# Reversing the order of the key chunks in the later passes of P V, in a fused attention and gated feed-forward kernel

## Chip, cores and metric

The kernel runs on one core of one Trainium2 chip. The metric is device time in microseconds (us), the median of several executions.

## What is computed

Block-causal attention (blocks of 64 positions) over a batch of 8, with 8 heads of size 64 and 576 positions, followed by a feed-forward layer whose hidden signal is gated by a convolution of width 3:

```
scores = np.where(block_i >= block_j, scale * q @ k.T, -1e9)
attn = exp(scores - max) / (sum + 1e-09)
x = (attn @ v) with the 8 heads side by side        # 576 x 512 for each batch
h = np.maximum(x @ w_in, 0.0)                       # 512 -> 1024
out = (h * sigmoid(conv3(h)) ) @ w_out              # 1024 -> 512
```

All is float32. The kernel reaches that precision with float32r matmuls by splitting an operand into a high part and a low part (the remainder) and adding the products of the parts.

## The kernel before

**Heads.** Heads are worked on in pairs, a "visit". The first batch is visited twice, once for its queries 0 to 255 (part "A") and once for its queries 256 to 575 (part "B"). The 28 pairs of the seven other batches are visited once, with all 576 queries (part None, "full-width" below). For each head: scores by 128 queries (L707 to L747), exponential and normalisation, transposes of the probabilities (L791), and then the product P V (L868), which is where the change is.

**Tiles of P V.** The transposed probabilities lie in `ptah` and `ptal` (high and low part, queries 0 to 255) and in `ptbh` and `ptbl` (queries 256 to 575). In `ptbh[:, c, :]` the 128 partitions are the keys of chunk c (c = 0 to 3, 128 keys each) and the 320 columns are queries 256 to 575. Only the last 64 queries see the last 64 keys (512 to 575). For them the corner of `ptbh` that chunk 3 leaves unused, `ptbh[:, 3, 0:64]`, is used: its partitions 0 to 63 hold the high part and 64 to 127 the low part. The values lie in `vv`, where the last 64 keys stand twice, in partitions 0 to 63 and 64 to 127 of chunk 4; columns 0 to 63 of `vv` are the high part ("h") and 64 to 127 the low part ("l"); "a" is both, 128 columns.

**Passes.** `stage_pv` makes a block of queries in one PSUM bank `tb` (tag "w" in the profile), by passes over the chunks. For a full-width head there are two passes: "a" with the high part of P (the stationary operand is `vv`, 128 columns wide) and "h" with the low part of P (64 columns wide). Parts A and B make three: "h", "l" with the high part of P, and "h" with the low part, all 64 columns wide. The stationary operand is loaded anew for each matmul. A full-width head has two blocks: queries 0 to 255 (chunks 0 and 1, moving 256 and 128 columns) and queries 256 to 575 (chunks 0 to 2 with 320 columns each, chunk 3 with 192). Before the change each pass goes from chunk 0 to the last, and the product of the last 64 keys (64 moving columns, the "tail", L875) stands right behind chunk 0 of each pass but the last. In the "l" pass of part B it reads 64 partitions in place of 128.

**Order of the work.** Nothing is ordered by the engines themselves. Every operation is given to a planner, `Plan.order`, with an engine, an assumed duration, a due time and what it depends on. The planner simulates the five engines, always takes the operation that can start first (due times break ties), and so writes out one fixed order for each engine. A pass over a block is one operation; for queries 256 to 575 it is cut in two halves, chunks 0 and 1, and chunks 2 and 3. The matmuls of the feed-forward layer (L936, L993) are "paced" operations which fill TensorE between the steps of the attention. Where the planner finds TensorE idle for longer than 0.45 us it inserts transposes of the identity (L1110) whose results nobody reads. The assumed duration of a matmul with n moving columns and m columns of stationary operand is `max(n / 2240, 2 * m / 2400) + 0.003` us. The waits between engines follow from what the instructions read and write, not from the planner's dependences.

Of the kernel before, what the change touches and what calls it, by code (L numbers as in the profile page):

```python
# [193 lines left out]
def kernel(  # L194
# [10 lines left out]
    nc = tc.nc  # L205
    B, H, S, D = q.shape
    DM, DFF = w_in.shape
    KC = conv_w.shape[0]
    P = 128
# [46 lines left out]
    def bank(tag):  # L256
        tag = {"tv": "w", "pt": "w"}.get(tag, tag)
        return pl.buf(psum[tag], [P, 512], F32, tag, NBANK[tag])
# [22 lines left out]
    def c_mm(n, m=P):  # L281
        return max(n / 2240.0, 2 * m / 2400.0) + 0.003

    def c_act(n, psum=True, ap=False, acc=False):
        return (0.051 if psum else 0.093) + n / 1200.0 + (0.093 if ap else 0) + (0.08 if acc else 0)

    def c_dve(n, fast=False, two_in=False):
        return 0.065 + n / (1920.0 if fast else 960.0) + (0.05 if two_in else 0.0)
# [559 lines left out]
    def stage_pv(vvd, hh, xt, x, at, part, chunk=lambda c: c, xx=None):  # L848
        early = part is not None
        vv, vdone = vvd  # L850
        o64 = 64 * hh
        done = []
        passes = (("h", 64, 0), ("l", 64, 0), ("h", 64, 1)) if early else (("a", P, 0), ("h", 64, 1))
        w = {"h": slice(0, D), "l": slice(D, P), "a": slice(0, P)}
        for qa, qb in {None: ((0, 256), (256, S)), "A": ((0, 256),), "B": ((256, S),)}[part]:
            tb = bank("tv")
            n = qb - qa
            pts = x[0] if qa == 0 else x[1]
            cs = [c for c in range(4) if 128 * c < qb]
            need = x[2] if qa == 0 else x[3]  # L860
            o = None
            for k, (ps_, m, lo) in enumerate(passes):
                halves = [cs] if qa == 0 else [cs[:2], cs[2:]]
                for z, half in enumerate(halves):
                    def mm(ps_=ps_, m=m, pm=pts[lo], pth=pts[0], half=half, k=k, tb=tb, qa=qa, qb=qb, cs=cs):
                        for c in half:
                            q0 = max(128 * c, qa)
                            nc.tensor.matmul(tb.ap[0:m, q0 - qa:qb - qa], vv.ap[:, chunk(c), hh, w[ps_]],  # L868
                                             pm.ap[:, 128 * c + q0:128 * c + qb] if qa == 0 else pm.ap[:, c, q0 - qa:],
                                             start=(k == 0 and c == 0),  # L870
                                             stop=(k == len(passes) - 1 and c == cs[-1]), skip_group_check=True)

                            if c == 0 and k < len(passes) - 1 and qb == S:
                                r = P if ps_ != "l" else 64
                                nc.tensor.matmul(tb.ap[0:m, 512 - qa:S - qa], vv.ap[0:r, 4, hh, w[ps_]],  # L875
                                                 pth.ap[0:r, 3, 0:64], start=False, stop=False, skip_group_check=True)

                    cost = sum(c_mm(qb - max(128 * c, qa), m) for c in half) + (c_mm(64, m) if k == 0 and 0 in half else 0)
                    deps = [o] + vdone + ([e[0] for e in need] if k == 0 else [])
                    deps += [e[1] for e in need] if lo else []  # L880
                    if qb == S:
                        deps += [need[-1][1]]
                    o = pl.op(PE, cost, mm, at + (0.3 if qa else 0), deps=deps, bufs=[vv, tb] + pts)

            def ev0(tb=tb, qa=qa, qb=qb, n=n):
                nc.scalar.activation(out=xt.ap[o64:o64 + 64, qa:qb], in_=tb.ap[0:64, 0:n], func=AF.Copy)  # L886

            def ev3(tb=tb, qa=qa, qb=qb, n=n):
                nc.vector.tensor_tensor(out=xt.ap[o64:o64 + 64, qa:qb], in0=tb.ap[64:128, 0:n],  # L889
                                        in1=xt.ap[o64:o64 + 64, qa:qb], op=ALU.add)  # L890

            def evh(tb=tb, qa=qa, qb=qb, n=n):
                nc.scalar.activation(out=xx[0].ap[o64:o64 + 64, qa:qb], in_=tb.ap[0:64, 0:n], func=AF.Copy)

            def evl(tb=tb, qa=qa, qb=qb, n=n):
                nc.vector.tensor_tensor(out=xx[1].ap[o64:o64 + 64, qa:qb], in0=tb.ap[0:64, 0:n],
                                        in1=xx[0].ap[o64:o64 + 64, qa:qb], op=ALU.subtract)

            if xx:
                o = pl.op(ACT, c_act(n) + 0.08, evh, at + 0.6, deps=[o], bufs=[tb, xx[0]])  # L900
                done.append(pl.op(DVE, c_dve(n, two_in=True) + 0.02, evl, at + 1.0, deps=[o], bufs=[tb] + list(xx)))
                continue
            o = pl.op(ACT, c_act(n) + 0.08, ev0, at + 0.6, deps=[o], bufs=[tb, xt])
            if not early:
                o = pl.op(DVE, c_dve(n, two_in=True) + 0.07, ev3, at + 1.0, deps=[o], bufs=[tb, xt])
            done.append(o)
        return done
# [164 lines left out]
    for i, (p, part) in enumerate(visits):  # L1072
# [8 lines left out]
        for hh in range(2):  # L1081
            n = 2 * i + hh
            b0 = base[n]
            sm = stage_s(ops, hh, b0, part, None)
            if hh == 0 and i + 1 < len(visits):
                nops = transposes(i + 1, b0 + ot)
                if i + 2 < len(visits) and i + 2 > NP:
                    fetch(i + 2, b0 + ot + NLEAD)
            x = stage_x(sm, hh, b0 + ox, part, x[4] if x else None)
            es += stage_pv(vvd[i], hh, xt, x, b0 + opv, part, (lambda c, p=p: 2 * (p % 2) + c) if part == "A" else lambda c: c, xs[p][:2] if part and XDIRECT else None)  # L1090
# [5 lines left out]
        if p % NP == NP - 1:  # L1096
            xb = [(xs[z][0], xs[z][1], list(xs[z][2])) for z in range(b * NP, b * NP + NP)]
            c = base[2 * i + 2] + opv + (OFA if part == "A" else OFB if part else OF)
# [4 lines left out]
            else:  # L1103
                for half in range(2):
                    c = ffn(b, HS * half, HS * half + HS, xb, c, H * SLOT / 2)
# [40 lines left out]
```

## Time and profile before

| | us |
|---|---|
| median of 3 runs | 825.06 (824.58 to 827.27) |
| the profiled execution's own time | 826.01 |
| its span, from the first to the last instruction | 824.2 |
| TensorE busy in it | 805.8 (98%) |

Busy times are those of the profile. A matmul's recorded duration runs from its start to the end of its results and overlaps the next one; how fast matmuls follow each other is read from their starts.

### The profile page before, as it was taken

What the parts mean: (1) busy time and instruction counts of PE and PEld (TensorE: products, weight loads), DVE (VectorE), ACT (ScalarE), POOL (GpSimd) and SP (SyncE); (2) the same over time, 40 slices, a digit from 0 to 9 for tenths busy, and PEclk for the clock granted to TensorE, in tenths of its full rate; (3) what the DMA queues carried; (4) which work ended last, traced back from release to release, by engine and by line L of the source; (5) the groups of instructions that cost most, each with busy time, mean ns of one, the idle gap of its engine ahead of it and who ended that gap; (6) DMA issues with size and microseconds to landing.
All of it is one profiled execution on the core that took longest, in us unless ns stands there. A gap on an engine that the chain in (4) does not pass through costs nothing.

```text
span 824.2 us, 17518 instructions
## 1 busy us (share of the span) xinstructions
PE 805.8 (98%) x5531; PEld 736.6 (89%) x5531; DVE 658.5 (80%) x1945; ACT 634.0 (77%) x1800; POOL 437.9 (53%) x579
## 2 busy tenths in 40 slices
PE   7999899999999999999999999999999999999997
PEld 6888778988999989999999989999999989999996
DVE  5899887998997967889797967889797977887541
ACT  5789887887896967878796967878796967877651
POOL 2456566564565645546555645546565645645421
PEclk9999999999999999999999999999999999999999
DMA  9364756556555544444556444445556434430001
GB/s 234 113 155 104 183 159 157 131 126 147 146 119 145 117 103 107 106 113 114 145 119 146 108 113 103 106 114 117 145 119 144 116 91 113 93 99 14 14 26 40
DMA packets 168096, 96.09 MB, mean 117 GB/s; under 512 B 136748, under 2 KB 142404, under 8 KB 168004
## 3 DMA queue, kind: packets, MB, share of 16 engines
q1 hardware_dynamic: 165924, 94.44, 47.3%
q8 instruction: 45, 0.74, 0.4%
q10 hardware_dynamic: 2080, 0.52, 0.4%
q14 instruction: 47, 0.39, 0.2%
HBM read 38.82 MB, written 9.44 MB: 59 GB/s over the span
## 4 chain that ended last, share of the span: by engine, by line
PE 90%; DVE 3%; SPq 2%; ACT 2%; DMA 2%; issue 1%; POOL 0%; ACTq 0%; DVEq 0%
PE f L936 24%; PE f L993 21%; PE w L868 12%; PE w L791 10%; PE s L709 5%; PE s L711 5%; PE w L582 4%; PE w L993 3%; PE s L747 3%; PE s L936 2%; PE s L1110 1%; DMA xh<-in_moe_w_out_dram 1%; SPq L372 1%; DMA kn<-in_k_dram 1%; DMA ka<-kh 1%
## 5 line engine op out<-in xcount | busy, mean ns | idle before, releaser
L682 POOL TENSOR_SCALAR p<-p,st 128x512 f32<-128x512 f32 (+4 forms) x260 | 144.3, 570 | 158.6 <-DVE st L676 73.1
L974 POOL TENSOR_TENSOR gl<-t,gh 128x288 fp32r<-128x288 f32 (+2 forms) x128 | 103.9, 816 | 127.4 <-ACT gh L971 101.2
L720 ACT ACTIVATE p<-s,st 128x128 f32<-128x128 f32 (+1 forms) x248 | 131.2, 529 | 36.2 <-DVE st L717 31.0
L791 PE MATMUL w<-ident,p 128*128 128x128 f32 (+1 forms) x800 | 126.6, 275 | 1.9 <-DVE kl L589 1.4
L717 DVE TENSOR_REDUCE st<-s 128x1 f32<-128x128 f32 (+1 forms) x248 | 120.4, 486 | 4.0
L801 ACT ACTIVATE ptbh<-w 128x512 fp32r<-128x512 f32 (+2 forms) x192 | 94.5, 509 | 26.5 <-PE w L791 25.5
L791 PEld LDWEIGHTS w<-ident,p 128*128 128x128 f32 (+1 forms) x800 | 95.3, 140 | 12.9 <-ACT p L688 1.9
L993 PE MATMUL f<-woh,gh 128*128 128x512 f32 x248 | 105.8, 427 | 0.0
L936 PE MATMUL f<-xh,wih 128*128 128x290 f32 (+2 forms) x480 | 101.7, 312 | 0.4 <-ACT stage L1003 0.3
L804 DVE TENSOR_TENSOR ptbl<-w,ptbh 128x512 fp32r<-128x512 f32 (+1 forms) x144 | 89.9, 633 | 14.8 <-ACT ptbh L801 14.3
L936 PE MATMUL f<-xh,wil 128*128 128x290 f32 (+2 forms) x480 | 99.2, 310 | 0.0
L993 PE MATMUL f<-woh,gl 128*128 128x512 f32 x248 | 98.2, 396 | 0.0
L993 PE MATMUL f<-wol,gh 128*128 128x512 f32 x248 | 98.1, 395 | 0.0
L936 PE MATMUL f<-xl,wih 128*128 128x290 f32 (+2 forms) x480 | 96.0, 305 | 0.0
L711 PE MATMUL s<-kl,qz 128*128 128x128 f32 (+1 forms) x240 | 78.0, 325 | 0.0
L936 PEld LDWEIGHTS f<-xh,wih 128*128 128x128 f32 x480 | 74.1, 189 | 3.9 <-DVE t L967 0.6
L955 DVE SCALAR_TENSOR_TENSOR t<-f,cw,t 128x287 f32<-128x287 f32 (+3 forms) x120 | 59.0, 492 | 20.6 <-ACT t L951 19.4
L936 PEld LDWEIGHTS f<-xl,wih 128*128 128x128 f32 x480 | 73.8, 190 | 0.8
L936 PEld LDWEIGHTS f<-xh,wil 128*128 128x128 f32 x480 | 73.2, 190 | 0.3
L889 DVE TENSOR_TENSOR xt<-w,xt 64x256 f32<-64x256 f32 x112 | 51.3, 460 | 27.2 <-ACT xt L886 24.6
L886 ACT ACTIVATE xt<-w 64x256 f32<-64x256 f32 x112 | 44.8, 402 | 23.0 <-PE w L868 18.4
L868 PE MATMUL w<-ptbh,vv 128*128 128x320 f32 (+3 forms) x288 | 62.3, 320 | 0.0
(161 smaller groups left out, 2054.7 us busy)
## 6 DMA issues: line engine op xcount, KB each, us to landing
kn<-in_k_dram SPq DMA_DIRECT2D x64, 144.0 KB, 2.9
ka<-kh SPq DMA_DIRECT2D x64, 144.0 KB, 2.7
kb<-kh SPq DMA_DIRECT2D x64, 144.0 KB, 2.6
out_dram<-stage SPq DMA_DIRECT2D x36, 256.0 KB, 2.3
vn<-in_v_dram SPq DMA_DIRECT2D x64, 128.0 KB, 2.6
qn<-in_q_dram SPq DMA_DIRECT2D x56, 144.0 KB, 2.7
qa<-qh SPq DMA_DIRECT2D x28, 144.0 KB, 3.1
qa<-ql SPq DMA_DIRECT2D x28, 144.0 KB, 3.1
```

The lines of the kernel that those rows point to most:

```text
L682: nc.gpsimd.tensor_scalar(out=pt.ap, in0=pt.ap, scalar1=st.ap[:, col:col + 1], scalar2=0.0, op0=ALU.mult, op1=ALU.add)
L711: nc.tensor.matmul(sb.ap[:, 0:nk], qz.ap[:, z:z + 128], kl.ap[:, 0:nk], start=False, stop=True)
L717: nc.vector.tensor_reduce(out=st.ap[:, i:i + 1], in_=sb.ap[:, 0:nk], op=ALU.max, axis=AX.X, negate=True)
L720: nc.scalar.activation(out=pt.ap[:, 0:nk], in_=sb.ap[:, 0:nk], func=AF.Exp, bias=st.ap[:, i:i + 1], accum_out=st.ap[:, 4 + 2 * i:5 + 2 * i])
L791: nc.tensor.matmul(tb.ap[0:kk, col:col + P], pb[x].ap[:, 128 * c:128 * c + kk], ident, start=(z == 0), stop=True, is_transpose=True, skip_ ...
L801: nc.scalar.activation(out=hi(), in_=src(), func=AF.Copy)
L804: nc.vector.tensor_tensor(out=lo(), in0=src(), in1=hi(), op=ALU.subtract)
L868: nc.tensor.matmul(tb.ap[0:m, q0 - qa:qb - qa], vv.ap[:, chunk(c), hh, w[ps_]], pm.ap[:, 128 * c + q0:128 * c + qb] if qa == 0 else pm.ap[ ...
L936: nc.tensor.matmul(fb.ap[:, 0:n2], wt[:, c, fs], xs[c][xi].ap[:, x0:x0 + n2], start=(n + c - c0 == 0), stop=(n + c - c0 == 3 * NCC - 1))
L955: nc.vector.scalar_tensor_tensor(out=t.ap[:, i0:no], in0=fb.ap[:, own + i0 - 1:own + no - 1], scalar=cw[:, f:f + 1], in1=t.ap[:, i0:no], o ...
L974: nc.gpsimd.tensor_tensor(out=gbuf[1].ap[:, f, carry:carry + no], in0=t.ap[:, 0:no], in1=gbuf[0].ap[:, f, carry:carry + no], op=ALU.subtract)
L993: nc.tensor.matmul(fb.ap[:, 0:DM], gbuf[a].ap[:, f, cs], w[:, f, :], start=(f == 0 and n == 0), stop=(f == NFC - 1 and n == 2))
```

## The change

In every pass but the first the chunks are taken from the last to the first, and the halves in reverse as well. The tail no longer stands behind chunk 0 of the same pass. It is the first matmul of the next pass, with the columns of `vv` that belong to the pass before (`wp`, `mp`), and always reads all 128 partitions. The number of matmuls is the same. The planner's durations follow: the tail is counted in the first half of each later pass, where it was counted in the first half of the first pass.

```diff
                 halves = [cs] if qa == 0 else [cs[:2], cs[2:]]
+                if k:
+                    halves = [h[::-1] for h in halves[::-1]]
                 for z, half in enumerate(halves):
-                    def mm(ps_=ps_, m=m, pm=pts[lo], pth=pts[0], half=half, k=k, tb=tb, qa=qa, qb=qb, cs=cs):
+                    tailed = k and z == 0 and qb == S
+                    def mm(ps_=ps_, m=m, pm=pts[lo], pth=pts[0], half=half, k=k, z=z, tb=tb, qa=qa, qb=qb, halves=halves,
+                           tailed=tailed):
+                        if tailed:
+                            wp, mp = passes[k - 1][:2]
+                            nc.tensor.matmul(tb.ap[0:mp, 512 - qa:S - qa], vv.ap[:, 4, hh, w[wp]],
+                                             pth.ap[:, 3, 0:64], start=False, stop=False, skip_group_check=True)
                         for c in half:
                             q0 = max(128 * c, qa)
                             nc.tensor.matmul(tb.ap[0:m, q0 - qa:qb - qa], vv.ap[:, chunk(c), hh, w[ps_]],
                                              pm.ap[:, 128 * c + q0:128 * c + qb] if qa == 0 else pm.ap[:, c, q0 - qa:],
                                              start=(k == 0 and c == 0),
-                                             stop=(k == len(passes) - 1 and c == cs[-1]), skip_group_check=True)
-
-                            if c == 0 and k < len(passes) - 1 and qb == S:
-                                r = P if ps_ != "l" else 64
-                                nc.tensor.matmul(tb.ap[0:m, 512 - qa:S - qa], vv.ap[0:r, 4, hh, w[ps_]],
-                                                 pth.ap[0:r, 3, 0:64], start=False, stop=False, skip_group_check=True)
-
-                    cost = sum(c_mm(qb - max(128 * c, qa), m) for c in half) + (c_mm(64, m) if k == 0 and 0 in half else 0)
+                                             stop=(k == len(passes) - 1 and z == len(halves) - 1 and c == half[-1]),
+                                             skip_group_check=True)
+
+                    cost = sum(c_mm(qb - max(128 * c, qa), m) for c in half) + (c_mm(64, m) if tailed else 0)
```

## Rows read from the trace of the kernel before

**Rows 1.** The page's head and its busy times.

```profile
span 824.2 us, 17518 instructions
...
PE 805.8 (98%) x5531; PEld 736.6 (89%) x5531; DVE 658.5 (80%) x1945; ACT 634.0 (77%) x1800; POOL 437.9 (53%) x579
```

**Rows 2.** Busy time by stretch: stretch, length, engines (instructions), clock, DMA share, GB/s.

```profile
240.00:400.00 160.00, 160.00 (x1087) 146.98 (x1086) 132.45 (x392) 125.19 (x363) 87.81 (x121) 1.00 0.49 117
...
320.00:340.00 20.00, 20.00 (x153) 19.35 (x152) 19.32 (x57) 19.05 (x57) 13.06 (x18) 1.00 0.54 124
```

**Rows 3.** Chain of waits, 240 to 760 us, then 60 to 135 us.

```profile
by line: PE f L936 28.3%; PE f L993 28.3%; PE w L868 13.2%; PE w L791 11.9%; PE s L711 5.4%; PE s L709 5.2%; PE w L582 4.1%; PE s L747 3.5%; PE w L875 0.3%
...
by line: PE w L868 13.4%; PE f L936 10.4%; PE w L791 6.9%; PE s L1110 6.8%; DMA kn<-in_k_dram 5.6%; DMA ka<-kh 5.5%; PE w L808 4.3%; issue 4.0%; PE f L993 3.9%; PE s L747 3.6%; DVE st L717 3.4%; PE s L709 3.3%; PE s L711 2.8%; ACT p L720 2.
...
88.30 4.19 DMA kn<-in_k_dram
```

**Rows 4.** Timeline of TensorE, one full-width head: start, us, instruction, count merged.

```profile
411.64 0.34 PE L868 MATMUL w<-ptal,vv 128*64 128x256 f32 x2
411.81 0.36 PE L868 MATMUL w<-ptbh,vv 128*128 128x320 f32 x1
412.01 0.19 PE L875 MATMUL w<-ptbh,vv 128*128 128x64 f32 x1
412.04 0.62 PE L868 MATMUL w<-ptbh,vv 128*128 128x320 f32 x3
...
412.27 0.40 PE L868 MATMUL w<-ptbh,vv 128*128 128x320 f32 x2
...
412.50 0.69 PE L868 MATMUL w<-ptbl,vv 128*64 128x320 f32 x4
413.03 0.46 PE L936 MATMUL f<-xh,wih 128*128 128x290 f32 x2
...
413.19 0.30 PE L936 MATMUL f<-xh,wih 128*128 128x290 f32 x1
```

**Rows 5.** Timeline of TensorE, another full-width head, between its two blocks.

```profile
423.11 0.49 PE L936 MATMUL f<-xl,wih 128*128 128x290 f32 x2
...
423.30 0.30 PE L936 MATMUL f<-xl,wih 128*128 128x290 f32 x1
423.44 0.32 PE L868 MATMUL w<-ptbh,vv 128*128 128x320 f32 x1
423.59 0.19 PE L875 MATMUL w<-ptbh,vv 128*128 128x64 f32 x1
```

**Rows 6.** Groups of TensorE by form: line, operation, form, count, busy us, mean ns.

```profile
L868 PE MATMUL w<-ptbh,vv 128*128 128x320 f32 x168 | 43.5, 347 | 0.0
L868 PE MATMUL w<-ptbl,vv 128*64 128x320 f32 x192 | 41.1, 312 | 0.0
```

**Rows 7.** Timeline of TensorE, a head of part B.

```profile
106.18 0.19 PE L875 MATMUL w<-ptbh,vv 128*64 128x64 f32 x1
106.21 0.71 PE L868 MATMUL w<-ptbh,vv 128*64 128x320 f32 x4
...
106.38 0.40 PE L868 MATMUL w<-ptbh,vv 128*64 128x320 f32 x2
...
106.61 0.31 PE L868 MATMUL w<-ptbh,vv 128*64 128x320 f32 x1
...
106.85 0.24 PE L875 MATMUL w<-ptbh,vv 64*64 64x64 f32 x1
107.02 0.36 PE L868 MATMUL w<-ptbh,vv 128*64 128x320 f32 x1
107.22 0.38 PE L791 MATMUL w<-ident,p 128*128 128x128 f32 x2
```

**Rows 8.** Timeline of TensorE: transposes, two matmuls of the feed-forward layer, a transpose.

```profile
413.52 0.51 PE L936 MATMUL f<-xh,wil 128*128 128x290 f32 x2
413.87 0.25 PE L582 MATMUL w<-ident,qn 96*128 96x96 f32 x1
```

## The prediction

> **What bounds the kernel now.** I read the page first. TensorE is busy for 98% of the span, and its weight loads (PEld) for 89% [rows 1]. These busy times overlap one another, so they don't say yet that TensorE sets the pace. The busy times by stretch come next: between 240 and 400 us TensorE is busy without a gap at a granted clock of 1.00, which is the 2.4 GHz level, while VectorE has 132 of 160 us and ScalarE 125 [rows 2]. The chain of waits settles it: from 240 to 760 us its named shares are all TensorE's, and 13.2% of it are P V matmuls on L868 [rows 3]. So in the stretch that holds most of the 56 full-width heads, a nanosecond saved on TensorE is a nanosecond of the kernel, as long as the other engines keep their slack. Before 135 us it is different: from 60 to 135 us TensorE's lines share the chain with DMA transfers, VectorE, ScalarE and filler transposes (L1110), and L868 has 13.4% of 75 us [rows 3].
>
> Since matmuls overlap, I read TensorE's pace from starts. What a matmul occupies is the time from its start to the next start, its "slot". In the full-width head of [rows 4], the four matmuls of pass "h" (three of 320 columns, one of 192) take 413.03 - 412.50 = 530 ns. Three of pass "a" (320, 320, 192) take 412.50 - 412.04 = 460 ns, of which the first has 412.27 - 412.04 = 230 and the others 230 together. From 3x + y = 530 and x + y = 230, a slot of 320 columns is 150 ns and one of 192 is 80 ns. The tail has a slot of 412.04 - 412.01 = 30 ns. So the one matmul behind the tail takes 230 in place of 150 ns, 80 too many.
>
> My reading: the next weights are loaded while the current matmul streams, and a matmul waits only for the part of its load that the matmul ahead of it does not cover. Behind a 30 ns tail, 80 ns are uncovered, so a load of 128 columns is about 80 + 30 = 110 ns. This can be tested elsewhere. The two matmuls of 256 and 128 columns in [rows 4] take 411.81 - 411.64 = 170 ns, so some 60 for the shorter one, and behind it a0 takes 412.01 - 411.81 = 200: 50 too many, and 50 + 60 is 110 again. In [rows 5] a0 stands behind a matmul of 290 columns and takes 423.59 - 423.44 = 150: nothing too many. There the feed-forward matmul behind the 128-column one has 423.30 - 423.11 = 190 where the next has 140. The averages agree: the 168 matmuls of 320 columns with 128-column weights last 347 ns, the 192 with 64-column weights 312 [rows 6]. 35 ns times 168 is 5.9 us, and 56 times 80 ns (all a1) plus 30 times 50 ns (the 30 heads whose a0 follows the first block at once) is 6.0 us. A load of 64 columns: the matmul behind part B's first tail takes 106.38 - 106.21 = 170, 20 too many, so about 50 ns.
>
> The Trainium skill ("TensorE: Matmul & The Clock Gate", section "LDWEIGHTS (loading the stationary operand)") gives columns divided by 1.2 in ns, so 107 and 53 ns, whatever the number of rows. The 110 and 50 of the trace agree on columns; by that page's figures the full-width sum below would be within 0.3 us of the one from rows.
>
> **The change, part by part.** No matmul is added or removed; what changes is which load stands behind which stream.
>
> *Full-width heads, queries 256 to 575 (56).* Removed: a1 no longer follows the tail, 80 ns. Added: the tail now follows a3, whose 80 ns cover all but 30 of its 110 ns load: 30 ns. Then h3 follows the tail, with a 64-column load of 50 behind 30: 20 ns. The pass now ends with 320 columns in place of 192, so whatever comes next has its load covered: [rows 4] shows 413.19 - 413.03 = 160 for the next matmul where 140 is normal. That is 20 ns where a matmul with 128-column weights follows, nothing where transposes do; between 0 and 20 I take 15. Net 80 - 30 - 20 + 15 = 45 ns.
>
> *Full-width heads, queries 0 to 255 (56).* Pass "h" now ends with 256 columns in place of 128. a1 and h1 are followed by a 64-column load, which 60 ns cover both ways. Removed is the 50 ns that the next operation waits, whether it is a0 of the other block [rows 4] or a feed-forward matmul [rows 5]. In the timeline 54 of 56 have such a successor; the bounds are 0 and 50, and I take 50.
>
> Together 95 ns times 56 is 5.3 us. All of it is TensorE time on the chain, in the stretch where nothing else is on it.
>
> *Part B (8 heads).* Here the tail of pass "l" reads 64 partitions and its load is not fetched ahead: the matmul before it takes 106.85 - 106.61 = 240 ns (90 too many), the tail itself 107.02 - 106.85 = 170 (140 too many), the matmul behind it 107.22 - 107.02 = 200 (50 too many) [rows 7]. With 128 partitions these 280 ns go. The matmul behind the first tail loses its 20 and two matmuls behind the moved tails gain 20 each, so 260 ns a head, 2.1 us in all. By the skill's rule just named, the number of rows does not matter, and this 2.1 us would be about nothing; the trace differs, with 170 against 30 ns. How much of it is on the path? L868 has 13.4% of 75 us = 10 us of the chain there [rows 3]; eight heads of some 2 us each (14 slots of about 150 ns) are about 17 us. So 0.6 of it: 1.2 us, with bounds 0 and 2.1.
>
> *Part A (8 heads).* At most 50 ns each, at the start, where much else is waited for: 0 to 0.4 us, and I take 0.
>
> *Waits.* The tail reads the last thing that is made of a head's probabilities. It stands later now, so its wait can only get shorter. The low-part pass starts with chunk 3 in place of 0, but needs the same evictions of queries 384 to 511, so it starts no earlier. The evictions of `tb` wait for the last matmul of the last pass as before. No DMA is added or moved by the edit itself.
>
> *The planner.* By its own formula the tail counts 0.056 us (64 columns) where it counted 0.110 in a full-width head, and twice 0.056 where it counted 0.056 once in part B. So the written-out order will shift from the first head of part B on. In the stretch bound by TensorE an order costs only through its neighbours: a feed-forward matmul behind a transpose takes 413.87 - 413.52 - 140 = 210 ns, 70 more than behind its like [rows 8]. Ten such places more or fewer are 0.7 us. Before 135 us a changed order can move waits on loads, of which the chain shows one of 4.19 us [rows 3]. Taken at 0, with 1.5 us either way.
>
> The sum: 5.3 + 1.2 = 6.5 us off. Against the profiled execution, 826.01 - 6.5 = 819.5 us; that execution was 0.95 us above the median of the runs, from which it is 818.6. I forecast 819.2 us.
>
> **Rivals.**
> 1. *Another engine becomes the bound.* Where attention is dense the others are near full: from 320 to 340 us VectorE is busy for 19.32 of 20 us and ScalarE for 19.05 [rows 2]. If half of each head's 95 ns ends in waits for them, 2.7 us are left plus part B's share: about 822 us. Against it: the chain of 520 us names none of them [rows 3]. At a whole loss, 825 us.
> 2. *The new order eats the gain in the middle.* It takes 60 to 90 more places where a matmul follows a transpose (70 ns each [rows 8]): 4 to 6 us, so 823 to 825 us.
> 3. *Loads are not covered at all, so order does not matter.* Then each matmul would pay its load and its stream in any order, and only the 64-partition tails would bring something: about 824 us. The trace speaks against it: a2 with a 128-column load takes 150 ns, not 150 + 110 [rows 4]. The skill's same page, section "Measured speedup vs the span model", says that loads overlap running matmuls only where the row groups differ. By that rule nothing here but the 64-row tail would overlap; the rows show otherwise, and only part B's 64-row tail behaves in a way that rule could touch.
> 4. *Slower.* The order shifts in part B, between 60 and 135 us, so that loads of q, k or their shifted copies come late, as the one of 4.19 us at 88.30 does [rows 3]. With a second one the kernel is still faster, 6.5 against 4.2; from the third on (8.4 more) it is slower: 827 us and above.
>
> **How the numbers follow.** About 0.3% (2.5 us) is what a measurement of this kernel can tell from no change. The forecast has 0.75, spread over 817 to 822 by part B's bounds (1.2 less, 0.9 more) and the planner's 1.5. Rival 1 has 0.09, two thirds of it faster than 822.6. Rival 2 has 0.08, rival 3 has 0.03, both within 0.3% mostly. Rival 4 has 0.05, of which 0.04 slower by over 0.3%. So faster 0.82, same 0.13, slower 0.05. The range of 816.5 to 823.0 takes in the forecast's own and most of rival 1.
>
> **What would show it.** In the profile after: the matmul behind a0 has a slot of 150 ns; the 168 matmuls of `ptbh` with 128-column weights last close to 312 to 320 ns on average; what follows a block's last pass has its normal slot; no 64-partition load is left, and the second tail of part B has a slot near 30. The chain from 240 to 760 us stays TensorE's. The prediction is wrong if those slots shrink and the span doesn't: then idle time of TensorE in the dense stretches (rival 1), longer slots behind transposes (rival 2), or longer DMA pieces on the chain before 135 us (rival 4) will show where it went.

## The result, and the profile after

The changed kernel takes 826.64 us (median of 22 runs, 825.14 to 828.88), the kernel before 824.76 us (22 runs beside it, 823.3 to 827.27). The ratio is 1.0019, with a 95% interval of 1.0012 to 1.0026: 1.6 us slower by the ratio, 1.9 by the medians. That is less than 0.3%, but clear of no change, and far from the forecast of 819.2 us. The profiled execution took 825.66 us, about 1 us less than the median, while that of before took 826.01, about 1 us more than its own; so the two traces differ by less than the kernels do, and the other way (spans of 823.8 against 824.2 us). One execution of the kernel before, beside later runs, took 1098.89 us at a granted clock of 0.65; it counts in no ratio and in nothing below.

Head of the page after, to set beside [rows 1]:

```profile
span 823.8 us, 17574 instructions
...
PE 803.7 (98%) x5550; PEld 734.1 (89%) x5550; DVE 655.7 (80%) x1945; ACT 633.8 (77%) x1800; POOL 436.7 (53%) x579
```

TensorE is 2.1 us less busy, although it has 19 matmuls more. The edit adds none: those are fillers (293 transposes of the identity in the trace, 274 before), which the planner inserts where it expects TensorE to idle. This is the first sign that the planner made another order.

A full-width head in the timeline of TensorE after, to set beside [rows 4]:

```profile
413.26 0.34 PE L880 MATMUL w<-ptah,vv 128*128 128x256 f32 x2
413.44 0.34 PE L880 MATMUL w<-ptal,vv 128*64 128x128 f32 x2
413.61 0.69 PE L880 MATMUL w<-ptbh,vv 128*128 128x320 f32 x4
414.14 0.22 PE L876 MATMUL w<-ptbh,vv 128*128 128x64 f32 x1
414.19 0.72 PE L880 MATMUL w<-ptbl,vv 128*64 128x192 f32 x4
414.75 0.44 PE L944 MATMUL f<-xh,wih 128*128 128x290 f32 x2
```

Pass "a" (three matmuls of 320 columns, one of 192) now takes 414.14 - 413.61 = 530 ns: nothing too many. The tail has a slot of 414.19 - 414.14 = 50 ns where 60 were forecast, and pass "h" takes 414.75 - 414.19 = 560, which is 30 more than 530 where 20 were forecast; together they cost the 50 ns that were forecast. The groups by form say the same of all heads, beside [rows 6]:

```profile
L880 PE MATMUL w<-ptbl,vv 128*64 128x320 f32 x192 | 39.4, 309 | 0.0
L880 PE MATMUL w<-ptbh,vv 128*128 128x320 f32 x168 | 35.4, 312 | 0.0
```

The 168 matmuls with 128-column weights went from 347 to 312 ns. So the edit does to the slots what was forecast. A head of part B, to set beside [rows 7]:

```profile
119.40 0.72 PE L880 MATMUL w<-ptbh,vv 128*64 128x192 f32 x4
119.96 0.48 PE L808 MATMUL w<-ptbh,nident 128*128 128x128 f32 x3
120.27 0.19 PE L876 MATMUL w<-ptbh,vv 128*64 128x64 f32 x1
120.30 0.71 PE L880 MATMUL w<-ptbl,vv 128*64 128x192 f32 x4
120.85 0.39 PE L1001 MATMUL f<-woh,gh 128*128 128x512 f32 x1
```

The second tail reads 128 partitions, and its slot is 120.30 - 120.27 = 30 ns where it was 170. The passes behind the first tail and behind the second take 560 and 550 ns, 30 and 20 more than 530, and nothing of the 280 ns is left.

Where the time is lost again shows when the same head is looked up in both traces. The first two lines are of the kernel before, the next fence is of the changed kernel:

```profile
259.90 0.28 PE L868 MATMUL w<-ptah,vv 128*128 128x256 f32 x1
...
737.56 0.28 PE L868 MATMUL w<-ptah,vv 128*128 128x256 f32 x1
```

```profile
262.52 0.28 PE L880 MATMUL w<-ptah,vv 128*128 128x256 f32 x1
...
737.46 0.28 PE L880 MATMUL w<-ptah,vv 128*128 128x256 f32 x1
```

The changed kernel is 2.6 us behind at the first of these heads and level at the last: it loses in the first 260 us and gains 2.7 us over the next 41 heads, 66 ns each. Busy times from 50 to 100 us (columns as in [rows 2]), first before, then after:

```profile
50.00:100.00 50.00, 46.20 (x356) 41.99 (x357) 45.91 (x140) 44.00 (x117) 32.36 (x31) 0.99 0.62 151
```

```profile
50.00:100.00 50.00, 41.85 (x329) 38.46 (x328) 44.45 (x129) 42.61 (x111) 29.47 (x29) 0.97 0.58 140
```

TensorE idles for 8.15 us of this stretch in place of 3.80. Between 140 and 260 us it idles for 2.31 us in place of 0.31; from 0 to 50 us and from 100 to 140 us it idles less than before, by 2.2 and 2.3 us (the fillers count as busy). What TensorE waited for between 50 and 100 us, after (its weight loads; waited for, us in total, times, longest):

```profile
PEld f L944 <- DVE t L975: 3.8, 3, 2.0
PEld s L709 <- ACT t L959: 2.1, 1, 2.1
PEld s L747 <- ACT p L720: 1.5, 1, 1.5
```

The same view of the kernel before has 0.2 us for the first of these, and as its longest another one:

```profile
PEld s L709 <- ACT p L761: 2.0, 1, 2.0
...
PEld f L936 <- DVE t L967: 0.2, 1, 0.2
```

Feed-forward matmuls of the first batch now wait for VectorE to finish with `t` (the gate's last product, which frees their PSUM bank), and scores wait for ScalarE. The edit touches none of these instructions. Only the order can have put them where they wait.

### The profile page after: what moved, and what is told of

It is laid out like the page before. It is cut to its first block, busy times and chain, and to the rows that moved or that the text cites. A ratio compares the mean times of both kernels' runs of the same rounds, so it can differ in the third digit from the quotient of the medians.

```text
span 823.8 us, 17574 instructions
## 1 busy us (share of the span) xinstructions
PE 803.7 (98%) x5550; PEld 734.1 (89%) x5550; DVE 655.7 (80%) x1945; ACT 633.8 (77%) x1800; POOL 436.7 (53%) x579
## 4 chain that ended last, share of the span: by engine, by line
PE 85%; DVE 5%; ACT 4%; SPq 2%; issue 1%; DMA 1%; DVEq 0%; ACTq 0%
PE f L944 22%; PE f L1001 21%; PE w L880 11%; PE w L791 10%; PE s L711 4%; PE s L709 4%; PE w L1001 3%; PE w L582 3%; PE s L747 3%; PE s L944 2%; PE s L1118 1%; ACT p L720 1%; DVE st L717 1%; DVE ptbl L804 1%; DMA xl<-in_moe_w_out_dram 1%
## 5 line engine op out<-in xcount | busy, mean ns | idle before, releaser
L791 PE MATMUL w<-ident,p 128*128 128x128 f32 (+1 forms) x800 | 124.5, 275 | 0.9 <-ACT p L688 0.5
L944 PE MATMUL f<-xh,wih 128*128 128x290 f32 (+2 forms) x480 | 98.6, 309 | 3.9 <-DVE t L975 3.5
L944 PE MATMUL f<-xl,wih 128*128 128x290 f32 (+2 forms) x480 | 92.5, 304 | 0.0
L959 ACT ACTIVATE t<-f,cw 128x288 f32<-128x288 f32 (+2 forms) x120 | 60.0, 501 | 4.6
```

The costliest lines, as they stand in the source:

```text
L791: nc.tensor.matmul(tb.ap[0:kk, col:col + P], pb[x].ap[:, 128 * c:128 * c + kk], ident, start=(z == 0), stop=True, is_transpose=True, skip_ ...
L944: nc.tensor.matmul(fb.ap[:, 0:n2], wt[:, c, fs], xs[c][xi].ap[:, x0:x0 + n2], start=(n + c - c0 == 0), stop=(n + c - c0 == 3 * NCC - 1))
L959: nc.scalar.activation(out=t.ap[:, 0:no], in_=fb.ap[:, own:own + no], func=AF.Copy, scale=cw[:, NFC + f:NFC + f + 1])
```

## The experiments

Each time below is a median, beside runs of the kernel before on the same chip; the ratio to before is given with its 95% interval.

**The two halves of the change apart.** The edit changes the matmuls, and it changes the durations that the planner is told. The first run keeps the new matmuls and gives the old durations:

```diff
-                    cost = sum(... for c in half) + (c_mm(64, m) if tailed else 0)
+                    was = cs if qa == 0 else (cs[:2], cs[2:])[z]
+                    cost = sum(... for c in was) + (c_mm(64, m) if k == 0 and 0 in was else 0)
```

> The matmuls of the change, but the planner is given the durations of the kernel before, so every engine has the order that it had before, but for the matmuls inside P V. Theory (the slots gain as forecast, and the planner's new order loses it again): the gain stands alone, 5.3 us from the 56 full-width heads and about 1.2 from part B, so about 818 us (817 to 820), and in 250 to 760 us some 4.4 us less than before. Rival (the saved TensorE time ends in waits for other engines, whatever the order): 824 to 826 us.

Measured: 821.38 us, ratio 0.9959 (0.9947 to 0.9971), 3.4 us less than before. The order of VectorE, ScalarE, GpSimd and of the DMAs is instruction for instruction that of the kernel before. The gain is there as soon as the order is left alone, but it is smaller than expected.

The second run does the reverse, old matmuls with the new durations:

```diff
-                    cost = sum(... for c in half) + (c_mm(64, m) if k == 0 and 0 in half else 0)
+                    will = half if k == 0 else halves[-1 - z][::-1]
+                    cost = sum(... for c in will) + (c_mm(64, m) if k and z == 0 and qb == S else 0)
```

> The matmuls of the kernel before, but the planner is given the durations of the change, so the order of every engine is that of the changed kernel. Theory: the order alone loses what the slots gained and 1.9 us more, so about 825 + 8 = 833 us (830 to 836). Rival (order does not matter, other engines bound): 824 to 827 us.

Measured: 831.71 us, ratio 1.0084 (1.0071 to 1.0097), 6.9 us more. The order of VectorE, ScalarE, GpSimd and of the DMAs is that of the changed kernel. The order alone costs that much, and it brings the waits of the changed kernel with it, with the matmuls of before (weight loads, 50 to 100 us):

```profile
PEld f L937 <- DVE t L968: 3.7, 3, 2.0
PEld s L709 <- ACT t L952: 2.4, 1, 2.4
PEld s L747 <- ACT p L720: 1.5, 1, 1.5
```

-3.4 and +6.9 would make +3.5, and the changed kernel has +1.6. Both halves have their sign; they add up only roughly.

**Part B's share.** The full-width heads alone changed (a condition `part is None` on the reversal and the moved tail; parts A and B have their old tail back), with the old durations:

> The change in the full-width heads alone (parts A and B keep their old matmuls, the tail of 64 partitions too), with the planner's old durations. Theory: 5.3 us less than before, 819.5 us (818.5 to 820.5), and the difference to the run with all heads changed is part B's share, 1.2 us (0 to 2.1). Rival: 824 to 826 us.

Measured: 820.96 us, ratio 0.9956 (0.9945 to 0.9968), half a us less gain than the range allowed. The run with all heads changed, on the same chip, is 0.4 us slower, so the new matmuls of parts A and B bring nothing that shows in the time; a gain of up to about 1 us cannot be told from none with five executions of each. Busy time from 50 to 140 us (PE, PEld, DVE, ACT, POOL), first with all parts changed, then with the full-width heads alone:

```profile
50.00:140.00 90.00, 81.55 (x625) 73.77 (x625) 79.86 (x244) 77.53 (x206) 57.84 (x60) 1.00 0.63 153
```

```profile
50.00:140.00 90.00, 83.59 (x625) 74.29 (x624) 79.69 (x244) 77.96 (x207) 58.32 (x60) 1.00 0.62 154
```

With the same 625 matmuls TensorE is busy for 2.0 us less, which is the forecast 8 x 260 ns. But the stretch holds the same work in the same 90 us: TensorE merely idles longer. Its longest pauses between 60 and 135 us (waited for, us in total, times, longest), with all parts changed:

```profile
PE s L709 <- ACT p L761: 1.8, 1, 1.8
PE w L791 <- DVE kl L589: 1.6, 1, 1.6
PE w L582 <- DMA kn<-in_k_dram: 1.4, 1, 1.4
PE s L747 <- DMA qdl<-ql: 1.2, 1, 1.2
```

The pauses before the two DMAs, with the full-width heads alone changed:

```profile
PE s L747 <- DMA qdl<-ql: 0.6, 1, 0.6
...
PE w L582 <- DMA kn<-in_k_dram: 0.5, 1, 0.5
```

These two pauses are longer by 0.6 and 0.9 us, which is 1.5 of the 2.0 us. The same pair of heads as above, in this kernel:

```profile
257.52 0.28 PE L880 MATMUL w<-ptah,vv 128*128 128x256 f32 x1
...
732.36 0.28 PE L880 MATMUL w<-ptah,vv 128*128 128x256 f32 x1
```

From one to the other it takes 474.84 us, against 477.66 before: 2.8 us over 41 heads, 69 ns each, the same as in the changed kernel (66). So the new order gives nothing back in the middle, and it takes nothing there either: with the old matmuls in the new order the same stretch takes 743.23 - 265.15 = 478.08 us, 0.4 us more than before.

**One term alone.** Only the low-part pass of queries 0 to 255 reversed, full-width heads, old durations:

```diff
+                if k and qa == 0 and part is None:
+                    halves = [cs[::-1]]
```

> The kernel before, in which only the low-part pass of the full-width heads' queries 0 to 255 is reversed (256 columns last in place of 128), with the planner's old durations. Theory: what follows a block no longer waits for 50 ns of its weight load; 54 of 56 blocks, 2.7 us in slots, of which three quarters arrive in the time as in the run with all full-width heads changed: 2.0 us less than before (1.4 to 2.7). Rival (the gain of the full-width heads comes from the moved tail alone): no change.

Measured: 823.2 us beside 824.39, ratio 0.9986 (0.9976 to 0.9995): 1.2 us less (0.4 to 2.0). Less than expected, but not nothing: the order of the last two matmuls of a pass alone is worth time. The trace has more of it: the same pair of heads is 734.77 - 258.65 = 476.12 us apart, 1.54 us less than before, or 38 ns a head. For 56 heads that would be some 2.1 us (an estimate), close to what was expected and just above the interval of the measured times.

**Which durations move the order.** The old formula counts a tail in the first pass of every block, also where there is none: for queries 0 to 255, so in all of part A. The new one does not. The changed kernel, with the old durations for parts A and B:

> The changed kernel, but parts A and B (the first batch) keep the planner's old durations; the full-width heads have the new ones. Theory: if the loss sits in the first 135 us, where waits are on the path and the order shifts from part A on, most of it goes: 820 to 822 us, of which the 2 us that were given back between 250 and 760 us stay. If the loss comes from the full-width heads' new durations, it stays at 825 to 827 us.

Measured: 820.22 us, ratio 0.9945 (0.9932 to 0.9958), 4.5 us less than before. The loss comes from the first batch's durations; the new ones of the full-width heads, whose order shifts too, do no harm that shows. For part A alone (`if part == "A"`), and for part B alone:

> The changed kernel, with the planner's old durations for part A alone. Theory (the loss comes from the order's shift in part A, whose durations alone are shorter from the first pass on): the loss goes, 820 to 822 us, and the waits of feed-forward matmuls on VectorE between 50 and 100 us are gone. Rival (it comes from part B's durations): 825 to 828 us, with those waits.

> The changed kernel, with the planner's old durations for part B alone. Theory (part A's shift is the cause): the loss stays, 825 to 828 us, with the waits on VectorE between 50 and 100 us. Rival (part B's durations): 820 to 822 us.

Measured: 822.09 us, ratio 0.9972 (0.9959 to 0.9985), without waits of a microsecond on VectorE's `t`; and 825.81 us, ratio 1.0015 (1.0003 to 1.0026), with 2.4 us of them between 50 and 250 us. TensorE idles for 3.45 us between 50 and 100 us in the first of these runs and for 8.38 us in the second, beside 3.80 before and 8.15 with the whole change. Part A's durations carry most of the loss.

Then the kernel before, with part A's phantom tail taken out of the planner's durations and nothing else changed:

```diff
-                    ... + (c_mm(64, m) if k == 0 and 0 in half else 0)
+                    ... + (c_mm(64, m) if k == 0 and 0 in half and part != "A" else 0)
```

> The kernel before with one thing of the change: the planner no longer counts a tail of 0.056 us in the first pass of part A, where there is none. No matmul changes. Theory (part A's shift carries most of the order's loss): 4 to 5 us slower than before, 828 to 830 us. Rival (the loss needs the other new durations as well): within 1 us of before.

Measured: 832.79 us, ratio 1.0106 (1.0087 to 1.0125): 8.7 us slower, twice what was expected and the largest effect of all runs, from 0.056 us less in the assumed duration of 8 operations. Its longest wait from 50 to 100 us is a new one ("issue" is time in which the engine waited for nothing that the profile shows); the second is one that the changed kernel has too:

```profile
PEld w L791 <- issue: 3.5, 1, 3.5
PEld s L709 <- ACT t L951: 2.2, 1, 2.2
```

And the kernel before, with the same operations counted as longer by 0.02 us:

```diff
+                    if part == "A" and k == 0:
+                        cost += 0.02
```

> The kernel before, in which the planner counts the first pass of each P V of part A as 0.02 us longer: no matmul changes, and the sign is the opposite of the change's. Theory (any shift of the order in the first batch moves the waits there, in either direction, and there is no rule in the size or sign of the duration): within 3 us of 825, and not equal to it: 822 to 829 us, with other waits in 50 to 140 us. Rival (durations too short are what harms, so longer ones do not): 824 to 826 us.

Measured: 828.44 us, ratio 1.0047 (1.0030 to 1.0065). Shorter or longer, the order that comes out is worse. There is no rule in the sign.

**A better version.** The kernel of the run with the first batch's old durations, and the tail one place later, behind the second matmul of the later pass:

```diff
-                        if tailed:
-                            ...
                         for c in half:
                             ...
+                            if tailed and c == half[-1]:
+                                wp, mp = passes[k - 1][:2]
+                                nc.tensor.matmul(tb.ap[0:mp, 512 - qa:S - qa], vv.ap[:, 4, hh, w[wp]], ...)
```

> The changed kernel with the old durations for parts A and B (the run of 820.2 us), and in each later pass the tail stands behind the second matmul of the first half, so that a 320-column matmul is ahead of its 128-column load. Theory (a matmul waits for what the stream ahead of it does not cover of its load): the tail's slot goes from 51 to 30 ns in the 56 full-width heads and the matmul behind it still pays 25 to 30, so 56 x 21 = 1.2 us less: about 819.0 us (818.3 to 819.8). Rival (the tail pays the same wherever it stands): 820.2 us.

Measured: 819.45 us beside 824.52, ratio 0.9939 (0.9921 to 0.9957), 5.0 us less than before. A head of it:

```profile
408.37 0.40 PE L876 MATMUL w<-ptbl,vv 128*64 128x192 f32 x2
408.61 0.20 PE L883 MATMUL w<-ptbh,vv 128*128 128x64 f32 x1
408.64 0.49 PE L876 MATMUL w<-ptbl,vv 128*64 128x320 f32 x2
408.97 0.43 PE L947 MATMUL f<-xh,wih 128*128 128x290 f32 x2
```

The tail's slot is 408.64 - 408.61 = 30 ns, as expected; the two matmuls behind it take 330 ns in place of 300. The step from 820.22 is 0.8 us across two sets of runs, which are uncertain by 1.5 and 1.1 us, so the step by itself is not shown by the times. It is by the traces. The same two heads, first in this kernel, then in the one without the step:

```profile
256.92 0.28 PE L876 MATMUL w<-ptah,vv 128*128 128x256 f32 x1
...
731.09 0.28 PE L876 MATMUL w<-ptah,vv 128*128 128x256 f32 x1
```

```profile
258.35 0.28 PE L880 MATMUL w<-ptah,vv 128*128 128x256 f32 x1
...
733.46 0.28 PE L880 MATMUL w<-ptah,vv 128*128 128x256 f32 x1
```

That is 474.17 against 475.11 us, 23 ns a head. The four traces with the tail in its first new place (the changed kernel, and the runs of 821.38, 820.96 and 820.22 us) have 474.84 to 475.11, so the step is clear of what differs between executions.

## Why the prediction was wrong

**What bounds the kernel** was read rightly. From 240 to 760 us the chain is TensorE's after the change as well:

```profile
by line: PE f L944 28.4%; PE f L1001 28.4%; PE w L880 12.7%; PE w L791 11.9%; PE s L711 5.4%; PE s L709 5.3%; PE w L582 4.0%; PE s L747 3.6%; PE w L876 0.4%
```

**The slots** were right to within 10 ns: 230 to 150 ns for the matmul behind a0's tail, the normal slot behind a finished block, 50 for the moved tail (60 forecast), 30 more for the matmul behind it in a full-width head (20 forecast), the 64-partition load's 280 ns gone. Rival 3, that loads are not covered at all, is out. The rule of the Trainium skill that it names ("TensorE: Matmul & The Clock Gate") stands in that page's section "The mechanism", not in the one given; the traces differ from it, since 320-column matmuls with 128-partition loads follow one another at 150 ns and it is the load from 64 partitions that was not covered.

**The full-width term, 5.3 us, was too large.** Measured by itself it is 3.6 us (2.6 to 4.5). Summing the slots between the two heads in the trace with the full-width heads alone changed, P V and the matmuls right behind it take 3.5 us less than before, 86 ns a head where I had 95. The rest of TensorE's matmuls take 0.7 us more in sum, of which 0.5 us are transposes of q and k, and 2.8 us remain, 69 ns a head. Waits of some 30 ns, too short to be listed, appear for instance where transposes of k follow scores. So of the 95 ns, 9 were too many in the slots and 17 went again in other matmuls. That is what rival 1 describes, at about a third of the size that I gave it, if another engine ends those waits. Which engine ends those waits stays open.

**Part B's 1.2 us did not arrive.** I took the share that L868 has on the chain as the share of a saving that arrives. The saving did happen on TensorE (2.0 us less busy) and the time stayed the same. In a stretch with such a mixed chain earlier matmuls only wait longer for what else is on it: 1.5 of the 2.0 us are found again in the pauses before a DMA of k and one of q.

**The step that failed** is the term "The planner", "Taken at 0, with 1.5 us either way". It cost 5 to 7 us, more than the whole gain, as the run of old matmuls in the new order (+6.9 us) and the run of new matmuls in the old order (-3.4) show. Without it the kernel takes 821.38 us, inside the forecast's range in spite of the other two terms. Two things were wrong in it. I wrote that the order shifts "from the first head of part B on"; the old formula counts a tail also in part A, so the order shifts there, and that shift alone is worth +8.7 us in the kernel before. And 1.5 us was a guess: the trace gave one load of 4.19 us as the price of a wait that may move, and several such waits can come at once. Rival 4 had the right kind of cause, waits that a shifted order moves, and about the right time, but the wrong waits: not late loads of q and k, but feed-forward matmuls and scores waiting for VectorE and ScalarE. Its place, 60 to 135 us, holds only in part: the idle time that was added lies between 50 and 100 us and, for 2.0 us, between 140 and 260 us. It got 0.05. Rival 2, a worse order in the middle, did not happen: old matmuls in the new order lose 0.4 us there, not 4 to 6.

Why the order of the kernel before is better than those of all three runs that changed only durations, in either direction, no run shows. It fits with constants that were chosen for that order, but this is argued, not shown.

## What to carry to other kernels

Where a planner writes out the order from assumed durations, an edit that touches a duration is two edits: make it once with the old durations, and give the new order a range of its own from a kernel whose durations alone were shifted. Read what a matmul costs from start to start, and put a short matmul where the stream ahead covers its weight load and the load behind it is small. A saving on an engine counts in full only in a stretch whose chain names that engine alone, and even there some of it came back as waits.

## What was not expected of the hardware

A load of weights from 64 partitions between loads from 128 was not fetched ahead of the running matmul, and neither was the load behind it. The weight loads (PEld) of the head of part B in [rows 7], before the change:

```profile
106.18 0.48 PEld L868 LDWEIGHTS w<-ptbh,vv 128*64 128x64 f32 x4
106.85 0.13 PEld L875 LDWEIGHTS w<-ptbh,vv 64*64 64x64 f32 x1 [0.19 <-issue]
107.02 0.13 PEld L868 LDWEIGHTS w<-ptbh,vv 128*64 128x64 f32 x1
```

The second and third start at 106.85 and 107.02 us, together with their own matmuls in [rows 7]. The slots are 240 and 170 ns where 150 and 30 are normal, and with the 50 ns of the matmul behind, one such load costs 280 ns; with 128 partitions they are gone.

In the trace of the changed kernel the granted clock of TensorE is 0.95 on average between 60 and 135 us, where it was 0.98 before, so part of that time passes at the lower of the two levels, 1.2 GHz. It does not explain the loss. The run with part A's old durations has 0.95 there too and is 2.3 us faster than before; the run with part B's old durations has 0.98 and keeps the loss. Over a whole execution the granted clock is 0.990 to 0.998 in the changed kernel and 0.991 to 1.000 in the kernel before, and the changed kernel's nine executions at 0.990 to 0.992 have a median of 826.40 us, its nine at 0.996 to 0.998 one of 826.89 us. What the clock adds to a single execution was not separated from the waits.
